# Projection stage of an attention and MLP kernel: Q and K tiles stored directly, weight splitting handed out from one paced list

## The chip, the cores and the metric

One NeuronCore of a Trainium2 chip runs the whole kernel. The metric is the device time of one execution in microseconds. Three runs of the kernel before gave 3447.6, 3449.01 and 3449.11 us, so its median is 3449.01 us.

## The reference, cut to what matters

The input x has 2048 rows of 1024 numbers. It is normalised, goes through an attention block of 32 heads and through an MLP with a Mish activation, and the two results are multiplied:

```python
xn = layernorm(x)
q, k, v = split(xn @ wqkv)                        # 32 heads of 32
s = softmax(q @ k.T * 32**-0.5) @ v, joined @ wo
h = xn @ w1 + b1                                  # 1024 -> 3584
g = silu((h * tanh(softplus(h))) @ w2)            # 3584 -> 1024
out = x + s * g
```

All tensors are float32.

## The kernel before

Every float32 operand of a product is split into a high part, rounded to the type that TensorE multiplies (`F32R`), and a low part, the rest. A product is then three matmuls (`THREE`, line 284). The high part is made by `copy` (line 273, ScalarE, shown as ACT) or by a copy on GpSimd (POOL); the low part by `low` (line 280), a subtraction on VectorE (DVE) or POOL. W2's products also go by sums and differences of its four blocks, seven tiles in place of eight (`w2_parts`, line 655).

The program has three stages before the long one: normalising x and the V projection (lines 368 to 525), then the **Q and K projection** (lines 677 to 719), and after it attention and MLP, whose order on every engine is set by a planner (`Plan`, line 82). The change lies in the Q and K projection alone.

That stage has 16 feature tiles f (even f is Q, odd f is K) with 4 column groups c each. I number the 64 groups as slots, 4f + c. In each slot `qk_group` (line 677) issues 24 matmuls of 128x512 into one PSUM bank, ACT copies the bank to the high half of a tile `st` (shown as qst, two buffers), DVE makes its low half, and ACT's queue stores the 512 KB to DRAM. The store is not issued by `qk_group` itself: it is put on the list `later` (line 49) and issued by `later.tick()` at the end of the same slot. PSUM has eight banks in one ring. From f = 12 on, each slot also has four matmuls of head 0's scores (`s_mm`, line 578), whose row maxima DVE takes.

Beside this, three things go on:

- In slots with c = 0, `qk_split` (line 482) splits the weights of the next f: two copies on ACT and two subtractions on DVE (names qkw). The raw weights for the f after that are loaded by ACT's queue (`qk_load`, line 476).
- In the first 14 f, `w2_parts(f, c)` gives POOL one step of W2's pair u = f: 2, 2, 2 and 1 tiles (`w2_part`, line 649). SP's queue stores each tile (w2s from pw) and, after step 3, loads the raw blocks for u + 2 (`w2_load`, line 645).
- In the first 10 f, at c = 3, `presplit` (line 630) loads half a tile of W1 on SP's queue; two ticks later POOL splits it and SP stores it (w1s from pw). There is one buffer for the raw half (praw) and six for the results (pw).

SP's queue also loads the stacked Q and K of head 0 at slot 32 and of head 1 at slot 57 (`load_head`, line 560, lines 707 to 711). Head 1's tiles take the place of W2's raw blocks (`stacks(early, 1)` and line 646 have the same tags).

Each engine issues its instructions in the order of the code. Across engines the program is emitted in an order that the compiler finds by its own timing of the engines. In that emitted order, every transfer of SP's and ACT's queues takes the next of eight completion semaphores in turn. So a transfer is started only when the eighth transfer ahead of it has landed, unless that one is known to have landed, and whichever queue it was on. In the program before, the store of slot 47 comes eight after the transfer of W2 tile (13, 1), and the store of slot 48 eight after that of tile (13, 6). The last W2 transfer, tile (13, 3), stands between the stores of slots 45 and 46.

Of the kernel before, what the change touches and what calls it, by code (L numbers as in the profile page):

```python
# [20 lines left out]
NC = S // 512  # L21
NT = S // P
FT = F // P
SCALE = DH ** -0.5
EPS = 1e-5

W1_0, W1_V = 4, 23
NS = H * NT
U = FT // 2

# [191 lines left out]
def body(ctx: ExitStack, tc: tile.TileContext, x, wqk, wv, wo, w1, b1, w2, out):  # L222
    nc = tc.nc
# [49 lines left out]
    def copy(out_, in_, scale=1.0):  # L273
        nc.scalar.activation(out_, in_, AF.Copy, scale=scale)  # L274

    def move(out_, in_, eng=None):

        (eng or nc.sync).dma_start(out_.bitcast(F32), in_.bitcast(F32))

    def low(eng, out_, in_, high):  # L280

        eng.tensor_tensor(out_, in_, high.bitcast(F32), ALU.subtract)  # L282
# [10 lines left out]
    later = Later()  # L293
# [148 lines left out]
    for t in range(2, NT + 2):  # L442
# [22 lines left out]
        if t > 7:  # L465
            c, k = t // 4 - 1, t % 4 * 2
# [9 lines left out]
    def qk_load(f):  # L476
        raws[f] = big.tile([P, KT, P], F32, tag="raw", name=f"qkraw{f}")
        (nc.scalar if f > 1 else nc.sync).dma_start(raws[f], wqk[f])
# [3 lines left out]
    def qk_split(f):  # L482
        qkw[f] = w_tile(f"qkw{f}")
        split_w(qkw[f], raws.pop(f))
# [50 lines left out]
    def stacks(pool_, i):  # L535
        stack_pool.append(pool_)
        qst.append(pool_.tile([P, S], F32R, tag=f"qstack{i}", name=f"qstack{i}"))
        kst.append(pool_.tile([P, S], F32R, tag=f"kstack{i}", name=f"kstack{i}"))
        if i == 0:
            nc.gpsimd.memset(qst[i][96:P, :].bitcast(F32), 0.0)  # L540
            move(zeros, qst[i][96:P, :])
            nc.vector.memset(kst[i][96:P, :].bitcast(F32), 0.0)
            nc.vector.memset(kst[i][96:98, :].bitcast(F32), 1.0)
# [16 lines left out]
    def load_head(h, parts=range(3)):  # L560
        r = slice(h % 4 * DH, h % 4 * DH + DH)
        q, k = qst[h % 3], kst[h % 3]
        if h > 2:
            move(q[96:98, :], zeros[0:2, :])
        elif h:
            move(q[96:P, :], zeros)
            move(k[96:P, :], kst[0][96:P, :])
        for i, (a, b) in enumerate(THREE):
            move(q[i * DH:(i + 1) * DH, :], qs[h // 4][a, r, :])
            move(k[i * DH:(i + 1) * DH, :], ks[h // 4][b, r, :])  # L570
# [7 lines left out]
    def s_mm(h, qt, kc):  # L578
        sp_ = ps1.tile([P, 512], F32, tag="ps", name=f"s{h}_{qt}_{kc}")
        nc.tensor.matmul(sp_, qst[h % 3][:, qt * P:(qt + 1) * P],  # L580
                         kst[h % 3][:, kc * 512:(kc + 1) * 512], start=True, stop=True)
        if qt % 4 == 0 and kc == 0:
            negm[h] = early.tile([P, 4, 4], F32, tag=f"mx{qt // 4 % 2}", name=f"mx{h}_{qt}")
        nc.vector.reduce_max(negm[h][:, qt % 4, kc:kc + 1], sp_, axis=AX.X)
        if qt % 4 == 3 and kc == 3 and qt < NT - 1:
            m_tail(h, qt // 4, negm[h])
# [28 lines left out]
    def load_w1(n):  # L615
        w1t[n] = w1p.tile([P, 2, KT // 2, P], F32R, tag="w1", name=f"w1_{n}", bufs=W1S)
        move(w1t[n], w1s[n // 2 % FT][:, n % 2])
# [7 lines left out]
    def pw_tile(name):  # L625
        pw_made.append(name)
        where, tag = ((w1p, "w1"), (sp, "pw"))[len(pw_made) % 2]
        return where.tile([P, 2, 512], F32R, tag=tag, name=name, bufs=3)

    def presplit():  # L630
        f, half = next(jobs)
        raw = sp.tile([P, 512], F32, tag="praw", name=f"praw{f}_{half}", bufs=1)
        nc.sync.dma_start(raw.rearrange("p (k f) -> p k f", f=P), w1[f][:, half * 4:half * 4 + 4])

        def split():
            w = pw_tile(f"pw{f}_{half}")
            nc.gpsimd.tensor_copy(w[:, 0], raw)
            low(nc.gpsimd, w[:, 1], raw, w[:, 0])
            later.at(1, lambda: move(w1s[f][:, half], w.rearrange("p a (k f) -> p a k f", f=P)))

        later.at(2, split)
# [3 lines left out]
    def w2_load(u):  # L645
        raw2[u] = early.tile([P, 4, 512], F32, tag=f"{'qk'[u % 2]}stack1", name=f"raw2_{u}")
        nc.sync.dma_start(raw2[u].rearrange("p (f d) n -> p f (d n)", f=2), w2[u])

    def w2_part(u, j, v):
        w = pw_tile(f"pw2_{u}_{j}")  # L650
        nc.gpsimd.tensor_copy(w[:, 0], v)  # L651
        low(nc.gpsimd, w[:, 1], v, w[:, 0])
        later.at(1, lambda: move(w2s[u][:, j], w))

    def w2_parts(u, step):
        b11, b12, b21, b22 = [raw2[u][:, i] for i in range(4)]
        if step == 0:
            raw2[u, "t"] = sp.tile([P, 512], F32, tag="tmp2", name=f"tmp2_{u}", bufs=1)
        tmp = raw2[u, "t"]

        def minus(a, b, out_):
            nc.gpsimd.tensor_tensor(out_, a, b, ALU.subtract)  # L662
            return out_

        if step == 0:
            w2_part(u, 0, b11)
            w2_part(u, 2, b21)
        elif step == 1:
            w2_part(u, 5, minus(b12, b11, tmp))
            w2_part(u, 1, minus(b22, b12, b12))  # L670
        elif step == 2:
            w2_part(u, 4, minus(b22, tmp, tmp))
            w2_part(u, 6, b22)
        else:
            w2_part(u, 3, minus(b21, tmp, tmp))

    def qk_group(f, c):
        w = qkw[f]
        ps = ps1.tile([P, 512], F32, tag="ps", name=f"qk{f}_{c}")
        n = 0  # L680
        for k in range(KT):
            for a, b in THREE:
                nc.tensor.matmul(ps, w[:, k // 4, a, k % 4], xc[c][:, b, k], start=n == 0, stop=n == 3 * KT - 1)  # L683
                n += 1
        st = sp.tile([P, 2, 512], F32R, tag="qst", name=f"qst{f}_{c}")
        copy(st[:, 0], ps)
        low(nc.vector, st[:, 1], ps, st[:, 0])
        dst = (qs, ks)[f % 2][f // 2].rearrange("h p n -> p h n")[:, :, c * 512:(c + 1) * 512]
        later.at(1, lambda: move(dst, st, nc.scalar))

    w2_load(0)
    w2_load(1)
# [1 line left out]
    for f in range(2 * KT):  # L694
        for c in range(NC):
            qk_group(f, c if f < 2 * KT - 1 else (c + 1) % NC)
            if f < U:
                w2_parts(f, c)
                if c == 3 and f + 2 < U:
                    later.at(1, lambda u=f + 2: w2_load(u))  # L700
            if c == 3 and f < 2 * (FT - W1_V):
                presplit()
            if c == 0 and f + 1 < 2 * KT:
                qk_split(f + 1)
                if f + 2 < 2 * KT:
                    later.at(1, lambda f=f + 2: qk_load(f))
            if f == 8 and c == 0:
                load_head(0)
            if f == 14 and c == 1:
                stacks(early, 1)  # L710
                load_head(1)
            if f >= 12:
                for kc in range(4):
                    s_mm(0, 4 * (f - 12) + c, kc)
            if f == 2 * KT - 1 and c == 1:
                load_w1(0)
                load_w1(1)
            later.tick()
# [23 lines left out]

    total = 2 * 4 * NS * MM + NC * FT * 45 * MM + NS * PV
    slot = total / NS

# [89 lines left out]
    def t_stream():  # L835
        pts = {}
        for T in range(NS):
            h, kt = divmod(T, NT)
# [554 lines left out]
    for c in range(NC):  # L1393
        for s in range(4):
# [3 lines left out]
            for dh in range(2):  # L1398
# [5 lines left out]
                if c:  # L1404
                    n = 2 * s + dh
# [53 lines left out]
```

## Time and profile before

| | |
|---|---|
| median of three runs | 3449.01 us |
| the profiled execution | 3453.82 us |
| its span, first to last instruction | 3452.0 us |
| mean granted TensorE clock | 0.992 |
| PE busy over the span | 3372.2 us (98%) |
| POOL busy over the span | 2794.2 us (81%) |
| first Q and K matmul | 219.90 us |
| last score matmul of the stage | 621.27 us |

PE is TensorE, PEld its weight loads, SPq and ACTq the issuing of transfers on the queues of SP and ACT. "Busy" counts the time of an engine's own instructions; a waiting engine is idle. In a timeline the bracket behind a line gives the idle time ahead of it and the instruction or transfer that ended it. Records start and end with overlaps of about a tenth of a microsecond, since matmuls are pipelined.

### The profile page before, as it was taken

How to read it: one execution, taken by the hardware profiler on the slowest of the kernel's cores; microseconds unless marked ns; L12 is line 12 of the kernel's file. 1: busy time of each engine (PE TensorE's matmuls, PEld its weight loads, DVE VectorE, ACT ScalarE, POOL GpSimd, SP SyncE). 2: the span in 40 equal slices, each digit the busy share in tenths (PEclk: the TensorE clock that was granted, in tenths of full speed). 3: DMA queues.
4: the chain of work that ended last, by engine and by line, in shares of the span. 5: the costliest groups of instructions: out<-in, count | busy, mean ns of one | idle time of the engine just before them, and what ended most of it. 6: DMA issues, size and time to landing. Idle time of an engine off the chain costs nothing.

```text
span 3452.0 us, 48687 instructions
## 1 busy us (share of the span) xinstructions
PE 3372.2 (98%) x17491; PEld 2474.5 (72%) x17491; DVE 2616.3 (76%) x4382; ACT 2017.9 (58%) x3360; POOL 2794.2 (81%) x1033
## 2 busy tenths in 40 slices
PE   8999998999999999999999999999999999999999
PEld 8998777777776667666776676666676666667587
DVE  6012215899999998888989988898999889996753
ACT  6111111576776766676766677666676677677621
POOL 2669891689888989899889889989988999989910
PEclk9999999999999999999999999999999999999999
DMA  9989994444555556545455664445555545546582
GB/s 334 324 303 365 348 354 165 130 139 144 152 157 152 149 167 198 152 127 161 141 150 144 195 182 143 129 138 150 153 152 188 174 138 158 151 154 193 167 308 86
DMA packets 255477, 639.92 MB, mean 185 GB/s; under 512 B 90026, under 2 KB 99242, under 8 KB 244906
## 3 DMA queue, kind: packets, MB, share of 16 engines
q1 hardware_dynamic: 233364, 587.52, 54.7%
q10 hardware_dynamic: 21872, 49.29, 3.9%
q8 instruction: 139, 2.28, 0.3%
q14 instruction: 102, 0.84, 0.1%
HBM read 474.97 MB, written 160.69 MB: 184 GB/s over the span
## 4 chain that ended last, share of the span: by engine, by line
PE 78%; POOL 8%; DVE 7%; DMA 4%; ACT 2%; issue 1%; SPq 0%; ACTq 0%; POOLq 0%; DVEq 0%
PE h L1008 16%; PE y L1149 13%; PE pv L897 12%; PE s L762 12%; PE t L849 12%; PE v L329 4%; PE op L1276 4%; POOL pw L282 3%; PE qk L683 2%; DVE mx L768 2%; POOL pw L651 1%; POOL tmp L662 1%; POOL z L878 1%; DMA praw<-in_B_w_dram 1%; DVE yacc L1172 1%
## 5 line engine op out<-in xcount | busy, mean ns | idle before, releaser
L878 POOL TENSOR_TENSOR z<-z,p 128x2048 f32<-128x2048 f32 x448 | 2067.2, 4614 | 75.8 <-ACT p L271 51.4
L271 ACT ACTIVATE p<-t,zero 128x512 f32<-128x512 f32 x2048 | 1365.9, 689 | 459.4 <-PE t L849 438.9
L768 DVE TENSOR_REDUCE mx<-s 128x1 f32<-128x512 f32 x1984 | 1281.3, 680 | 69.6 <-PE s L762 66.9
L849 PE MATMUL t<-qstack,kstack 128*128 128x512 f32 x2048 | 792.1, 394 | 2.1 <-ACT p L271 0.9
L762 PE MATMUL s<-kstack,qstack 128*128 128x512 f32 x1984 | 756.7, 398 | 16.3 <-DMA kstack<-ks 4.8
L1008 PE MATMUL h<-xr,w 128*128 128x512 f32 x2016 | 678.1, 391 | 1.6 <-DVE aw L282 0.6
L1172 DVE TENSOR_TENSOR yacc<-yacc,y 128x512 f32<-128x512 f32 x728 | 491.2, 678 | 39.6 <-PE y L1149 36.4
L762 PEld LDWEIGHTS s<-kstack,qstack 128*128 128x128 f32 x1984 | 367.7, 188 | 162.0 <-issue 29.9
L849 PEld LDWEIGHTS t<-qstack,kstack 128*128 128x128 f32 x2048 | 382.0, 188 | 127.2 <-issue 28.5
L897 PE MATMUL pv<-p,v 128*32 128x512 f32 x4096 | 467.0, 596 | 0.9 <-ACT p L271 0.6
L1008 PEld LDWEIGHTS h<-xr,w 128*128 128x128 f32 x2016 | 378.6, 188 | 84.7 <-DVE aw L282 2.1
L683 PE MATMUL qk<-xc,qkw 128*128 128x512 f32 x1536 | 362.5, 397 | 12.5 <-ACT qkw L274 9.0
L683 PEld LDWEIGHTS qk<-xc,qkw 128*128 128x128 f32 x1536 | 293.7, 192 | 78.5 <-ACT qkw L274 10.7
L878 POOL TENSOR_TENSOR z<-p,p 128x2048 f32<-128x2048 f32 x32 | 147.7, 4617 | 231.2 <-ACT p L271 120.7
L897 PEld LDWEIGHTS pv<-p,v 128*32 128x32 f32 x4096 | 120.1, 110 | 277.4 <-issue 247.9
L282 DVE TENSOR_TENSOR qst<-qk,qst 128x512 fp32r<-128x512 f32 x64 | 44.2, 691 | 283.0 <-ACT qst L274 283.0
L274 ACT ACTIVATE qst<-qk 128x512 fp32r<-128x512 f32 x64 | 38.3, 598 | 345.7 <-PE qk L683 120.5
L1149 PE MATMUL y<-w,az 128*128 128x512 f32 x672 | 232.3, 395 | 5.7 <-POOL az L282 2.7
L1149 PE MATMUL y<-w,ay 128*128 128x512 f32 x672 | 228.1, 393 | 3.4 <-ACT ay L274 1.3
L1149 PE MATMUL y<-w,ax 128*128 128x512 f32 x672 | 225.6, 392 | 3.1 <-DMA w<-w2s 1.1
L1008 PE MATMUL h<-xc,w 128*128 128x512 f32 x672 | 225.3, 391 | 0.0
L329 PE MATMUL v<-vw,xc 128*128 128x256 f32 x1536 | 192.6, 286 | 5.8 <-DVE xc L282 3.7
(123 smaller groups left out, 3662.9 us busy)
## 6 DMA issues: line engine op xcount, KB each, us to landing
w<-w2s SPq DMA_DIRECT2D x392, 512.0 KB
w<-w1s SPq DMA_DIRECT2D x224, 512.0 KB
w2s<-pw SPq DMA_DIRECT2D x98, 512.0 KB
qstack<-qs SPq DMA_DIRECT2D x96, 256.0 KB
kstack<-ks SPq DMA_DIRECT2D x96, 256.0 KB
x<-in_A_x_dram SPq DMA_DIRECT2D x32, 512.0 KB
qs<-qst ACTq DMA_DIRECT2D x32, 512.0 KB
ks<-qst ACTq DMA_DIRECT2D x32, 512.0 KB
```

Source lines behind the costliest of these rows:

```text
L271: nc.scalar.activation(out_, in_, fn, bias=zero if bias is None else bias, scale=scale)
L282: eng.tensor_tensor(out_, in_, high.bitcast(F32), ALU.subtract)
L329: nc.tensor.matmul(ps[:, :256], xc[t // 4][:, a, k, (t % 4) * P:(t % 4 + 1) * P], w[:, b, k], start=n == 0, stop=n == 3 * KT - 1)
L683: nc.tensor.matmul(ps, w[:, k // 4, a, k % 4], xc[c][:, b, k], start=n == 0, stop=n == 3 * KT - 1)
L762: nc.tensor.matmul(sp_, qst[h % 3][:, qt * P:(qt + 1) * P], kst[h % 3][:, kc * 512:(kc + 1) * 512], start=True, stop=True)
L768: nc.vector.reduce_max(tiles["mx"][:, qt, kc:kc + 1], tiles[qt, kc], axis=AX.X)
L849: nc.tensor.matmul(tp, kst[h % 3][:, kt * P:(kt + 1) * P], qst[h % 3][:, c * 512:(c + 1) * 512], start=True, stop=True)
L878: nc.gpsimd.tensor_tensor(zs[h], pts[T - 1] if kt == 1 else zs[h], pts[T], ALU.add)
L897: nc.tensor.matmul(t["b"][c * DH:(c + 1) * DH, :], vt[h][:, k, :], pts[T - kt + k][:, c * 512:(c + 1) * 512], start=k == kt - size + 1, st ...
L1008: nc.tensor.matmul(t["h"], w1t[m_][:, a, k % 4], xts_[c][:, b, k], start=i == 0, stop=i == 3 * KT - 1)
L1149: nc.tensor.matmul(t["y"], acts[B, kind][:, p, half * 256 + s * P:half * 256 + (s + 1) * P], w2t[m_][:, q], start=i == 0, stop=i == 2)
L1172: nc.vector.tensor_tensor(ya, ya, t["y"], ALU.subtract)
```

## The change

The store of a Q or K tile is issued in `qk_group`, straight behind the copy and the subtraction, and no longer at the tick. W2's steps and W1's halves stand in one list `todo`, each with a place, its running cost over `PACE` = 1.85: a step costs its number of tiles, a half of W1 costs 1. In a slot all jobs are taken whose place is at or before the slot's number. The cost is 14 x 7 + 10 = 108 in all, so the last job falls due by slot 58; before, the last step was at slot 55. Head 1's loads move from slot 57 to slot 60.

```diff
+PACE = 1.85
...
+    todo, cost = [], 0.0
+    for u in range(U):
+        for step, n in enumerate((2, 2, 2, 1)):
+            def job(u=u, step=step):
+                w2_parts(u, step)
+                if step == 3 and u + 2 < U:
+                    later.at(1, lambda: w2_load(u + 2))
+            todo.append((cost / PACE, job))
+            cost += n
+        if u < 2 * (FT - W1_V):
+            todo.append((cost / PACE, presplit))
+            cost += 1
...
-        later.at(1, lambda: move(dst, st, nc.scalar))
+        move(dst, st, nc.scalar)
...
-            if f < U:
-                w2_parts(f, c)
-                if c == 3 and f + 2 < U:
-                    later.at(1, lambda u=f + 2: w2_load(u))
-            if c == 3 and f < 2 * (FT - W1_V):
-                presplit()
+            while todo and todo[0][0] <= f * NC + c:
+                todo.pop(0)[1]()
...
-            if f == 14 and c == 1:
+            if f == 15 and c == 0:
                 stacks(early, 1)
                 load_head(1)
```

## Rows read from the trace of the kernel before

**Rows 1.** Busy time by stretch: engines, granted clock, DMA share, GB/s.

```profile
core 0: us, PE busy (x) PEld busy (x) DVE busy (x) ACT busy (x) POOL busy (x), PEclk, DMA share, GB/s
226.96:530.02 303.06, 278.25 (x1179) 225.27 (x1178) 65.47 (x78) 41.45 (x73) 281.90 (x272) 0.96 0.96 347
538.46:621.11 82.65, 82.65 (x366) 68.43 (x365) 43.80 (x78) 10.40 (x21) 0.00 (x0) 1.00 0.37 124
...
275.00:300.00 25.00, 25.00 (x112) 20.70 (x111) 6.00 (x7) 3.56 (x7) 23.96 (x24) 1.00 1.02 394
```

**Rows 2.** Timeline of PE: start, length, line, operation [idle before, and what ended it].

```profile
219.90 152.51 PE L683 MATMUL qk<-xc,qkw 128*128 128x512 f32 x672
...
525.41 0.80 PE L580 MATMUL s<-kstack,qstack 128*128 128x512 f32 x1 [6.64 <-DVE qst L282]
...
529.44 8.28 PE L683 MATMUL qk<-xc,qkw 128*128 128x512 f32 x24
...
538.46 5.60 PE L683 MATMUL qk<-xc,qkw 128*128 128x512 f32 x24
...
544.81 5.60 PE L683 MATMUL qk<-xc,qkw 128*128 128x512 f32 x24
...
620.20 1.07 PE L580 MATMUL s<-kstack,qstack 128*128 128x512 f32 x4
```

**Rows 3.** Waits from 226 to 531 us: waiter, releaser, total, times, longest.

```profile
ACT qst L274 <- DMA w2s<-pw: 77.9, 13, 9.7
ACT qst L274 <- DMA ks<-qst: 61.0, 11, 11.6
...
PE s L580 <- DVE qst L282: 9.7, 2, 6.6
PE qk L683 <- ACT qkw L274: 9.0, 4, 4.0
...
POOL pw L651 <- DMA w2s<-pw: 5.8, 1, 5.8
...
POOL pw L637 <- DMA praw<-in_B_w_dram: 3.0, 3, 1.9
```

**Rows 4.** Timeline of ACT and of its queue, about slots 44 and 48.

```profile
494.47 0.60 ACT L274 ACTIVATE qst<-qk 128x512 fp32r<-128x512 f32 x1 [6.20 <-DMA w2s<-pw]
494.97 1.14 ACT L274 ACTIVATE qkw<-qkraw 128x512 fp32r<-128x512 f32 x2
502.03 0.40 ACTq L278 DMA_DIRECT2D ks<-qst  x1
...
524.03 0.60 ACT L274 ACTIVATE qst<-qk 128x512 fp32r<-128x512 f32 x1 [6.84 <-DMA w2s<-pw]
524.53 1.14 ACT L274 ACTIVATE qkw<-qkraw 128x512 fp32r<-128x512 f32 x2
528.97 0.37 ACTq L278 DMA_DIRECT2D qs<-qst  x1
```

**Rows 5.** Timeline of POOL: the list's first job and its end.

```profile
226.96 1.00 POOL L651 CAST pw<-raw 128x512 fp32r<-128x512 f32 x1 [16.06 <-DVE qst L282]
...
524.70 1.27 POOL L282 TENSOR_TENSOR pw<-raw,pw 128x512 fp32r<-128x512 f32 x1
...
528.74 1.28 POOL L282 TENSOR_TENSOR pw<-tmp,pw 128x512 fp32r<-128x512 f32 x1
```

**Rows 6.** Timeline of DVE behind slot 48's copy.

```profile
525.27 2.92 DVE L282 TENSOR_TENSOR qkw<-qkraw,qkw 128x512 fp32r<-128x512 f32 x2
528.11 2.47 DVE L584 TENSOR_REDUCE mx<-s 128x1 f32<-128x512 f32 x4
```

**Rows 7.** Timeline of SP's queue: head 0's loads, and W2's last stores.

```profile
398.67 0.73 SPq L278 DMA_DIRECT2D qstack<-qs  x1
...
413.15 1.84 SPq L278 DMA_DIRECT2D w2s<-pw  x2
...
492.98 37.38 SPq L278 DMA_DIRECT2D w2s<-pw  x14
```

## The prediction

> **What bounds the kernel now.** I read the busy time by stretch first, to find where PE is not full, then PE's timeline, then the waits of that stretch, then ACT's, POOL's, DVE's and SP's timelines at its end. PE is the bound over the whole span, so a microsecond that PE loses in the Q and K stage is a microsecond of the kernel. From 538 us on PE is full with a DMA share of 0.37; while POOL works on its list, from 226.96 to 530.02, PE has 278.25 of 303.06 us and the DMA share is 0.96 [rows 1]. The stage loses its time under the list.
>
> How much: 28 groups in 152.51 us make 5.447 us each, and with four score matmuls a slot takes 544.81 - 538.46 = 6.35 us [rows 2]. Undisturbed, 48 x 5.447 + 16 x 6.35 = 363.0 us would lead from 219.90 to 582.9. The stage ends at 620.20 + 1.07 = 621.3 [rows 2]: **38.4 us are lost**, all before 538.
>
> What takes them: PE waits little by name, 9.0 us for split weights and 9.7 for a freed bank, but ACT waits 77.9 us, in 13 places, on transfers of W2 tiles, and 61.0 on stores of K [rows 3]. A Q or K store neither reads nor writes W2's tiles; what ties them is the turn of the eight semaphores. So ACT can't be further than POOL's list lets it, and PE, eight banks ahead at most, stands still when ACT does. ACT evacuates slot 44 at 494.47 [rows 4] (counted back from the last evacuation); undisturbed that would be 219.90 + 45 x 5.447 = 465.0. It is 29.5 us late. Slot 48 is copied at 524.03 [rows 4], PE goes on at 525.41, starts slot 50 at 529.44 and never waits again [rows 2]. The list's last product ends at 530.02 [rows 5]. The end of the stage is therefore the list's end, plus the slots that stand behind it in the emitted order.
>
> **Is the list held by the slots?** This decides the change. POOL's 303.06 us hold 281.90 of work [rows 1]; of the other 21.2, waits make 5.8 + 3.0 = 8.8 [rows 3], and the gaps between 272 instructions 12.4. No wait is on ACT, DVE or PE once the list has started. (The wait ahead of the first job, 16.06 us [rows 5], I put down to the load of its raw data: the code gives that job nothing to wait for on DVE.) And W2's last 14 stores, which the code puts in slots 48 to 55, start at 492.98 [rows 7], when ACT is at slot 44 [rows 4]: POOL is four slots ahead of the place at which the code gives it the work. The code's slots do not hold POOL; its own 294 us of work and gaps do. A list with other due slots gives POOL the same instructions in nearly the same order, and the compiler's timing again lets it run ahead.
>
> **The change part by part.**
>
> *Store at once, c other than 0 (48 or 49 slots).* Between copy and tick ACT has no other work there: 0. In four slots with f of 12 or more a small copy of the row maxima now follows the store and not the reverse; PE needs it no sooner than nine ticks later: 0.
>
> *Store at once, c = 0 (15 slots).* The two copies for the next weights, 1.14 us, used to go ahead of the store; now they stand behind it, and behind its wait. The raw load behind them moves too, by nothing that was not there. Cover: the weights are needed three slots later, 16.3 us. Where ACT is later than that, the cover is gone, as at slots 44 and 48. At slot 44 the store starts at 502.03 and the copies at 494.97 [rows 4], so the copies would come up to 7.4 us later; PE would start slot 48 that much later, but slots 49 and 50 must wait for ACT's evacuations anyway, so it is hidden under the stand at 525.41. At slot 48 it is not hidden: DVE must split those weights (2.92 us) before it takes the maxima of slot 48 [rows 6], and the bank of that maximum is what PE waits for ahead of slot 50. Upper end: the copies start at 528.97 + 0.37 and not at 524.53 [rows 4], +4.8 us. Lower end: the store finds its semaphore free and waits for DVE's half alone, to about 525.35, +1.2. Below that there is nothing, since the copies went first before. The store, emitted sooner, should stand one or two transfers further ahead and so wait for the W2 tile before: 281.90 us of work over 108 tiles and halves are 2.6 us each. I take 4.8 - 2.6 = **+2.2**.
>
> The Trainium skill (DMA: Bandwidth & Descriptors, "Issuing engines are not separate DMA queues") says that the engine on which a transfer is started saves only the sequencer's time to start it, small beside the transfer. By it this part is worth 0 and the sum 2.2 lower; the rows disagree, since a start here was held for 3.6 us and for 6.2 while its own record takes 0.4.
>
> *The paced list.* The work is the same 98 W2 tiles and 10 halves of W1: 0 for POOL's 294 us. Its 8.8 us of waits can fall: a half of W1 is split up to a slot later after its load (3.0 us at stake); head 0's loads stand between two other W2 stores on SP's queue. They held W2's stores from 398.67 to 413.15 [rows 7] and through them POOL for 5.8. They still stand among W2's stores, about six tiles sooner, so I keep the 5.8 and take the 3.0 away: **-3.0**, ends -8.8 and 0.
>
> *Head 1's loads.* On SP's queue they stand behind all W2 stores before and after, with nothing between: 0.
>
> *Order of the transfers.* Which W2 transfer stands eight ahead of a given store changes. If the list ends one slot sooner or later among the stores, one slot more or fewer is left behind it: 6.35 us either way, unknown in sign; I take 0. Bytes and matmuls are unchanged.
>
> Sum: 2.2 - 3.0 = -0.8 against the profiled execution's 3453.82 us (span 3452.0 and 1.8 around it). That execution is 4.8 above the median, so the forecast is 3449.01 - 0.8 = **3448.2 us**. About 0.2%, or 6.9 us, is what a measurement of this kernel can tell from no change.
>
> **The rivals.**
>
> *The pace holds.* If the emitted order does follow the due slots, the list ends behind slot 58, and each store stands behind W2 tiles that POOL finished long ago. 58.4 slots are 48 x 5.447 + 10.4 x 6.35 = 327.5 us, for 294 of POOL. For it: 38.4 us lie there to be had. Against it: POOL's lead over the code. The DMA engines would limit it: they moved 347 GB/s at a share of 0.96 [rows 1], 361 at a full one; 303.06 us at 347 are 105.2 MB, ten more stores and two weight loads of 0.52 MB make 111.4, over 327.5 us 340 GB/s, a share of 0.94. At such shares waits remain; I leave a quarter, 10 us: 3449 - 28 = **3421**, between 3411 and 3430. Where 394 GB/s were moved (1.02) [rows 1], PE did not stop yet.
>
> *ACT's queue becomes the stop: slower.* At c = 0 the store's wait now holds the next weights. If the stand at 525.41 does not hide slot 44's 7.4 us, PE comes to slot 48 late as well: 7.4 + 4.8 = 12.2, **3461**; with one more group at a low clock (the first after the stand took 8.28 and not 5.60 us [rows 2]) 3464. It decides from the point at which ACT is over 16.3 us late, which it was, 29.5, at slot 44. Against it: PE's banks are full there, so it would have stood anyway.
>
> *Nothing moves.* If the compiler's order comes out the same but for single places, the terms above shrink to the first one: 3449 to 3452, inside the forecast.
>
> **How the numbers follow.** Forecast's mechanism, own range 3440 to 3458 (the terms' ends and a slot either way, not all at once): 0.60; of it 0.44 lies within 0.2%, 0.10 below, 0.06 above. Pace holds: 0.20. ACT's queue stops PE: 0.15. Something else: 0.05, near even. Faster 0.32, the same 0.44, slower 0.24. The range that should hold it 8 times in 10 goes into both rivals: 3422 to 3463.
>
> **What would show it.** Right: POOL's list again takes 300 us or so without waits on ACT or PE; ACT's waits on w2s stay near 78 us; the stage ends within a slot of 621; the qkw copies of slot 48 start behind its store. The pace holds, if the list ends near 545 us and ACT's waits on w2s go below 30. The rival on ACT's queue, if PE's wait for qkw grows from 9.0 to over 20 and the stage ends beyond 630. If another stage than this one changes by over 3 us, I have missed a coupling.

## The result, and the profile after

The changed kernel takes **3463.9 us**, the median of five runs (3462.05 to 3466.74), against 3449.11 us of the kernel before beside it. The ratio is 1.0043 with a 95% interval of 1.0028 to 1.0058: **slower by 14.8 us, 0.43%**. I had forecast 3448.2 us and no change, and the range ended at 3463. The profiled execution took 3463.9 us, its span is 3462.1.

Busy time by stretch of the changed kernel: the first stretch is POOL's list from its first job to its end, the second the slots behind it. It answers to [rows 1].

```profile
core 0: us, PE busy (x) PEld busy (x) DVE busy (x) ACT busy (x) POOL busy (x), PEclk, DMA share, GB/s
226.85:534.51 307.66, 276.77 (x1177) 224.81 (x1175) 64.03 (x72) 42.58 (x72) 280.57 (x272) 0.95 0.93 342
547.30:630.30 83.00, 83.00 (x369) 68.75 (x367) 43.62 (x76) 10.83 (x22) 0.00 (x0) 1.00 0.32 116
```

POOL's work is what it was, 272 instructions and 280.57 us, but the list takes 307.66 us where it took 303.06. PE now leaves 307.66 - 276.77 = 30.9 us of the stretch empty, before 24.8. Behind the list PE is full again.

PE's timeline of the changed kernel about slot 48, and its end of the stage (start, length; in brackets the idle time ahead and what ended it). It answers to [rows 2].

```profile
527.45 0.80 PE L582 MATMUL s<-kstack,qstack 128*128 128x512 f32 x1 [4.58 <-DVE qst L284]
531.61 0.80 PE L582 MATMUL s<-kstack,qstack 128*128 128x512 f32 x1 [3.37 <-DVE qst L284]
537.83 0.79 PE L582 MATMUL s<-kstack,qstack 128*128 128x512 f32 x1 [5.42 <-DVE mx L586]
538.42 8.33 PE L698 MATMUL qk<-xc,qkw 128*128 128x512 f32 x24
...
629.24 1.07 PE L582 MATMUL s<-kstack,qstack 128*128 128x512 f32 x4
```

Slot 50 starts at 538.42, 9.0 us later than at 529.44, and the stage ends at 630.3, 9.0 us later than at 621.3. The last stand before it (a wait of PE), 5.42 us for a row maximum, is one that I had named. In the kernel before it was 2.64 us:

```profile
528.84 0.79 PE L580 MATMUL s<-kstack,qstack 128*128 128x512 f32 x1 [2.64 <-DVE mx L584]
```

Two parts make the 9.0. **The list ends later**: its last product starts at 533.25 and takes 1.26, so it ends at 534.51 and not at 530.02, +4.5:

```profile
533.25 1.26 POOL L284 TENSOR_TENSOR pw<-tmp,pw 128x512 fp32r<-128x512 f32 x1
```

**The tail is longer**: from the list's end to the stage's end 95.8 us, before 91.25, +4.55. The two need different causes, and the next two views have them.

Waits of the changed kernel from 226 to 535 us (waiter, releaser, total, times, longest), as [rows 3].

```profile
ACT qst L276 <- DMA w2s<-pw: 68.3, 14, 7.3
...
PE qk L698 <- ACT qkw L276: 18.6, 4, 6.9
...
ACT qst L276 <- DMA w1s<-pw: 14.2, 1, 14.2
POOL pw L639 <- DMA praw<-in_B_w_dram: 13.8, 4, 5.3
...
ACT qkw L276 <- DMA w2s<-pw: 9.6, 2, 7.2
...
POOL pw L653 <- DMA w1s<-pw: 1.0, 1, 1.0
```

POOL's wait for the raw half of W1 is 13.8 us where it was 3.0; its wait of 5.8 for a W2 store is gone and 1.0 for a W1 store has come. Waits of 8.8 us have become 14.8. ACT's weight copies now wait on W2's transfers themselves, 9.6 us; no such line stood there before.

Timelines of the changed kernel at slot 48, ACT and its queue, then DVE; they answer to [rows 4] and [rows 6].

```profile
530.24 0.60 ACT L276 ACTIVATE qst<-qk 128x512 fp32r<-128x512 f32 x1 [3.57 <-DMA w2s<-pw]
534.77 0.39 ACTq L280 DMA_DIRECT2D qs<-qst  x1
535.21 1.15 ACT L276 ACTIVATE qkw<-qkraw 128x512 fp32r<-128x512 f32 x2 [4.38 <-DMA w2s<-pw]
...
535.88 1.29 DVE L284 TENSOR_TENSOR qkw<-qkraw,qkw 128x512 fp32r<-128x512 f32 x2 [4.32 <-ACT qkw L276]
537.09 2.48 DVE L586 TENSOR_REDUCE mx<-s 128x1 f32<-128x512 f32 x4
```

The copies start at 535.21, 0.44 us behind the store and 4.97 behind the evacuation; before it was 0.50 behind the evacuation (524.03 to 524.53). DVE can take the weights' low half only then, and the row maximum at 537.09 after that.

### The profile page after: what moved, and what is told of

The parts are those of the page before. It is cut to its first block, busy times and chain, and to the rows that moved or that the text cites. A ratio compares the mean times of both kernels' runs of the same rounds, so it can differ in the third digit from the quotient of the medians.

```text
span 3462.1 us, 48685 instructions
## 1 busy us (share of the span) xinstructions
PE 3371.6 (97%) x17491; PEld 2473.6 (71%) x17491; DVE 2619.2 (76%) x4382; ACT 2020.3 (58%) x3360; POOL 2792.6 (81%) x1033
## 5 line engine op out<-in xcount | busy, mean ns | idle before, releaser
L773 PE MATMUL s<-kstack,qstack 128*128 128x512 f32 x1984 | 755.8, 397 | 15.6 <-DMA kstack<-ks 5.9
L698 PE MATMUL qk<-xc,qkw 128*128 128x512 f32 x1536 | 362.5, 397 | 20.8 <-ACT qkw L276 18.6
```

The lines of the kernel that those rows point to most:

```text
L773: nc.tensor.matmul(sp_, qst[h % 3][:, qt * P:(qt + 1) * P], kst[h % 3][:, kc * 512:(kc + 1) * 512], start=True, stop=True)
```

## The experiments

Twelve runs were made, one of them of the kernel before once more. Each time stands beside the kernel before on the same chip. For the table I split the stage's time at the list's end in each profile: "list" is from the start of POOL's first tile to the end of its last, "tail" from there to the end of the stage's last score matmul.

| kernel | time, us (before beside it) | ratio, 95% interval | list | tail | span behind the stage |
|---|---|---|---|---|---|
| before | 3449.11 | | 303.06 | 91.25 | 2830.7 |
| before, second profile | 3448.67 (3450.14) | 0.9990 to 1.0008 | 302.06 | 92.37 | 2826.2 |
| changed | 3463.90 (3449.11) | 1.0028 to 1.0058 | 307.66 | 95.80 | 2831.8 |
| store at once alone | 3454.07 (3448.33) | 1.0005 to 1.0024 | 300.87 | 94.88 | 2828.8 |
| store at once, c = 0 | 3454.19 (3450.14) | 1.0002 to 1.0020 | 300.35 | 95.07 | 2826.4 |
| store at once, c = 1, 2, 3 | 3450.52 (3450.14) | 0.9993 to 1.0011 | 301.84 | 90.89 | 2825.9 |
| list alone | 3458.25 (3448.33) | 1.0018 to 1.0039 | 310.62 | 91.25 | 2829.9 |
| changed, half of W1 first | 3451.61 (3448.33) | 1.0001 to 1.0019 | 299.54 | 94.48 | 2829.1 |

### The two parts apart

The store alone, in the kernel before:

```diff
-        later.at(1, lambda: move(dst, st, nc.scalar))
+        move(dst, st, nc.scalar)
```

> Only the store is moved; W2 and W1 are handed out as before. Theory (the emitted order ties the stores to POOL's list, and the list's end sets the stage's end): POOL's list ends as before, near 530 us, with some 9 us of waits; the copies of slot 48's weights stand behind its store's wait, so PE goes on some 4.5 us later than before. Stage end near 626, time 3452 to 3456 us, a third of the whole loss. Rival (stores started at once crowd W2's transfers, and that is the whole loss): 3462 to 3466 us with the list ending near 534. Second rival (the store is harmless, the list is all): 3449 us, stage end 621.

3454.07 us, +5.7 (1.7 to 8.3 by the interval), as expected. In the profile the list is shorter and the tail longer than before: the list ends at 527.1 us and not near 530, the stage at 622.0 and not near 626. PE's last stand is the changed kernel's, 5.42 us for a row maximum.

The list alone, in the changed kernel:

```diff
-        move(dst, st, nc.scalar)
+        later.at(1, lambda: move(dst, st, nc.scalar))
```

> Only the list is paced; the store stays at the tick. Theory: W1's raw halves stand behind W2's raw blocks on SP's queue in some places, POOL waits 10 us or more for them, the list ends near 534.5 us, the stage near 626, time 3453 to 3459 us. Rival (the store is the whole loss): 3449 us, list end near 530. Second rival (the list is the whole loss): 3462 to 3466 us.

3458.25 us, +9.9 (6.2 to 13.4), as expected, with the list ending at 537.7 and the stage at 629.0, both 3 us later than I had said. The tail is that of before, 91.25 (the second profile of the kernel before has 92.37); the list is 310.62 us. Together the two parts give +15.6, the change +14.8: within their intervals they add up, so each part can be explained by itself.

### The list: what stands ahead of the half of W1

SP's queue in the kernel before, and in the changed kernel, at the same half (praw), the same raw blocks of W2 (raw) and the W2 store ahead of them (w2s); below each, POOL as it takes that half:

```profile
287.17 0.88 SPq L633 DMA_DIRECT2D praw<-in_B_w_dram  x1
...
290.02 0.32 SPq L278 DMA_DIRECT2D w2s<-pw  x1
290.38 0.90 SPq L647 DMA_DIRECT2D raw<-in_B_w_dram  x1
...
294.12 1.07 POOL L637 CAST pw<-praw 128x512 fp32r<-128x512 f32 x1
```

```profile
284.83 5.53 SPq L280 DMA_DIRECT2D w2s<-pw  x3
...
290.40 0.43 SPq L649 DMA_DIRECT2D raw<-in_B_w_dram  x1
290.88 0.79 SPq L635 DMA_DIRECT2D praw<-in_B_w_dram  x1
...
298.74 0.61 POOL L639 CAST pw<-praw 128x512 fp32r<-128x512 f32 x1 [4.86 <-DMA praw<-in_B_w_dram]
```

In the code before, both loads were due at c = 3, the half at once and W2's blocks one tick later. In the list the half has its own place behind step 3, often a slot later, and six of its ten loads now start behind the 1 MB of W2's blocks and the W2 store ahead of those, which SP holds until POOL has made its tile. POOL, which takes its jobs in the emitted order, reached four of these six halves before they had landed. At the half shown, the store is started by 290.4 us in both kernels. Before, the half's load had started ahead of it, and POOL came for the half 6.95 us after that start without a wait. Now the load starts 3.7 us later, at 290.88, and POOL comes at 293.88, only 3.0 us after the start, and waits 4.86: the half takes 7.86 us to land. So most of this wait is the later start; of the transfer itself, at most some 1 us more than the 6.95 that were enough before, the 1 MB may be the reason, which no run shows by itself. The test puts the half ahead of step 3, and so ahead of both, in the changed kernel:

```diff
         for step, n in enumerate((2, 2, 2, 1)):
+            if step == 3 and u < 2 * (FT - W1_V):
+                todo.append((cost / PACE, presplit))
+                cost += 1
...
-        if u < 2 * (FT - W1_V):
-            todo.append((cost / PACE, presplit))
-            cost += 1
```

> The changed kernel with each W1 half put ahead of W2's step 3 in the list, so that its raw load is issued ahead of the 1 MB load of W2's raw blocks. Same work. Theory: POOL's waits for these halves fall from 13.8 to under 5 us, the list ends 6 to 10 us sooner (525 to 529), and the stage with it: 3454 to 3458 us. Rival (the waits for the halves are not on the path, POOL's lateness is made up later): as the changed kernel, 3462 to 3466 us.

3451.61 us, some 12 us of the 14.8 back and more than I had expected. All ten halves go ahead of the raw blocks again. Waits from 226 to 527 us of this kernel:

```profile
POOL pw L639 <- DMA praw<-in_B_w_dram: 5.6, 1, 5.6
...
POOL pw L653 <- DMA w1s<-pw: 1.0, 1, 1.0
```

The wait is down to one of 5.6 us, at 407 us, with head 0's loads ahead of the half on SP's queue. The list takes 299.54 us, 8.1 less than in the changed kernel, while the tail keeps its 94.48.

### The store: which slots carry its cost

In the kernel before, stored at once only where c = 0, and only where it is not (the line of the diff above under `if first:`, and under `if not first:`, with the old line in the other branch):

> Before, with the store at once in the slots with c = 0 alone (there the two weight copies then stand behind the store and its wait), at the tick elsewhere. Theory A (the cost of storing at once lies in these copies: they hold DVE's halves of the weights, those hold the row maxima, and PE waits for the bank): all of the cost of the run with the store alone, +4 to +7 us against before, and PE's wait for a row maximum near 5.4 us as there. Theory B (the cost lies in the changed order of all the transfers): 0 to +2 us.

> Before, with the store at once in the slots with c = 1, 2, 3, at the tick where c = 0. Theory A: ACT has nothing between copy and tick there, so nothing changes: within 2 us of before, PE's wait for a row maximum as before (2.6 us). Theory B: +4 to +6 us.

+4.1 us (0.7 to 6.9) and +0.4 us (-2.4 to 3.8), beside the same runs of the kernel before. PE's last stands before slot 50, first with c = 0 at once, then with the others at once:

```profile
530.95 0.80 PE L580 MATMUL s<-kstack,qstack 128*128 128x512 f32 x1 [5.42 <-DVE mx L584]
```

```profile
527.64 0.80 PE L580 MATMUL s<-kstack,qstack 128*128 128x512 f32 x1 [2.65 <-DVE mx L584]
```

The cost is in the slots with c = 0, where the weight copies stand behind the store. Over all profiles of kernels without the gate that comes below, the tail is 91.4 us with these stores at the tick (four profiles, 90.89 to 92.37) and 95.3 with them at once (six, 94.48 to 95.93, two of them further down): **+3.9**. Theory B, the order of the transfers, does not fit these tails and stands. But the loss is not all seen in the stage: with the store at once alone, and with c = 0 alone, the list is shorter and the stage ends at 622.0 and 622.7 us, only 0.2 and 0.9 behind the 621.8 that the two profiles of the kernel before have on the mean, where the medians are 5.7 and 4.1 longer.

> The kernel before, once more, for a second profile of it: the first came from an execution 4.7 us above the median. If that surplus lies in the Q and K stage (transfers that meet otherwise from one execution to the next), a profile at the median shows the stage ending near 617 us and the rest as before; if it lies elsewhere, the stage ends near 621 again. As a kernel: the same time as before, within 2 us.

The second profile of the kernel before comes from an execution 1.8 us above its median and ends its stage at 622.4, not near 617: the 4.7 us by which the first execution was above its median do not show in the stage.

### What the pace would be worth: a gate

My rival "the pace holds" needed POOL to follow the slots, which the code does not make it do. So I made it: DVE copies one column of a slot's low half into a small tile, and POOL copies that column before it takes the slot's jobs.

```diff
+    token = early.tile([P, 64], F32, name="token")
+    gate = early.tile([P, 1], F32, name="gate")
...
         low(nc.vector, st[:, 1], ps, st[:, 0])
+        nc.vector.tensor_copy(token[:, 4 * f + slot:4 * f + slot + 1], st[:, 1, 511:512].bitcast(F32))
...
+            if todo and todo[0][0] <= f * NC + c:
+                nc.gpsimd.tensor_copy(gate, token[:, 4 * f + c:4 * f + c + 1])
             while todo and todo[0][0] <= f * NC + c:
```

> The changed kernel, and POOL is held to the slots: DVE writes one column of a token behind each slot's low half, and POOL copies it ahead of the slot's jobs (some 50 added instructions of 128x1 on POOL, 64 on DVE). The emitted order then has the list's end behind slot 58 and every store ahead of the W2 tiles of its own slot. Theory: ACT's waits on W2 transfers nearly vanish, PE's stands too; the stage ends between 583 and 602 us, time 3420 to 3437 us. Rival (the DMA engines are the bound, 0.95 busy under the list): ACT's waits turn into waits on its own stores, stage end near 620, 3445 to 3455 us. Second rival (the token makes POOL wait for slots and the list ends late, head 1's loads with it): a new stand behind the stage, gain under 10 us.

3448.25 us, ratio 0.9991 to 1.0008: no faster than before, where I had expected 3420 to 3437. But the stage ended at 583.9 us, 46 earlier than in the changed kernel, and PE did not stand in it. 30 to 36 us were lost behind the stage: 2862.1 us of span there, where all kernels of the table have 2826 to 2832. What differs there is the place of tiles: `token` and `gate` stand in a pool with the stacks of Q and K, and the stacks of heads 0 and 2 and the stage's buffers moved by 288 bytes (the tiles' own 260, rounded up). The next four kernels take this apart. In the first the column lies in `pad2`, a tile of 48 columns that is there already:

```diff
-    nc.vector.memset(early.tile([P, 48], F32, name="pad2"), 0.0)
+    pad2 = early.tile([P, 48], F32, name="pad2")
+    nc.vector.memset(pad2, 0.0)
...
+        i = slot % 40
+        nc.vector.tensor_copy(pad2[:, i:i + 1], st[:, 1, 511:512].bitcast(F32))
...
+            if todo and todo[0][0] <= slot:
+                nc.gpsimd.tensor_copy(pad2[:, 47:48], pad2[:, slot % 40:slot % 40 + 1])
```

> After, with the gate as in the run before (POOL takes a slot's jobs only behind that slot's low half, through one column that DVE copies), but the columns lie in the 48-column tile that stands there already, so no tile's place in SBUF moves. Theory A (the gate removes the stands, and what the first gate lost behind the stage, 33 us, came from the 260 bytes by which its two new tiles moved everything behind them): the stage ends near 584 again and the rest is as in the changed kernel, 3463.9 - (630.3 - 583.7) = 3417 us, down to 3448.3 - (621.3 - 583.7) = 3411; matmuls behind the stage come every 0.2265 us again. Theory B (a PE that has not stood in the stage runs the rest slower, or the emitted order of the rest changed): the stage ends near 584 and the time stays near 3448, matmuls behind the stage every 0.232 us.

> After, with the two tiles of the first gate (64 columns and 1 column) allocated at the same place and cleared once by DVE, and no gate. Theory A (the place of the tiles costs the time): the stage ends near 630 as in the changed kernel, and the rest loses some 33 us: 3463.9 + 33 = 3497 us, at least 3490. Theory B (the place does not matter): 3463.9 us, within 4.

The gate in `pad2`: **3419.37 us**, ratio 0.9906 (0.9891 to 0.9920), with the stage ending at 587.1. The two tiles without a gate: 3493.91 us against 3452.14, 0.0082 of a ratio above the changed kernel, some 28 us, with the stage ending at 631.1, as in the changed kernel. The gate is worth the stage's time and the tiles cost what it had given back.

> Before, with the gate of e5_gate_pad at its own slots (W2's steps at 4u + c, halves of W1 at c = 3), the store at the tick. Theory A (POOL's lead over the code is what costs the 38 us, the even pace costs or gives little): the stage ends at 583 to 592, PE waits for little, 3411 to 3420 us. Theory B (the even pace is needed as well: eight tiles in four slots of 21.8 us are 20.8 us of POOL's work, and with the halves of W1 POOL falls behind the slots again): stage end 600 to 615, 3428 to 3443 us.

3416.04 us, ratio 0.9899 (0.9884 to 0.9914): the old list at its old slots, gated, does as well as the even one. The pace of 1.85 is not needed once POOL can't run ahead.

> e5_gate_pad with the store back at the tick, so that in slots with c = 0 the weight copies stand ahead of the store again. Theory A (a store costs the copies behind it only what it waits, and under the gate it waits for next to nothing): as e5_gate_pad within 3 us. Theory B (storing at once costs by itself, 4 to 6 us as in the run with the store alone): 4 to 6 us faster than e5_gate_pad.

**3414.20 us, ratio 0.9886 (0.9869 to 0.9902): the lowest median, and faster than both kernels**; the gated old list is not told apart from it. It is 5.2 us below the gate with the store at once, whose four runs all lie above these four. Theory B's number came, with theory A's place: there the gate does not make the c = 0 stores free. It can, though: in the profile of the first gate, which stores at once too, PE does not stand at slot 50 and needs 364.3 us for the stage. PE at slot 50 with the store at once, then PE in the whole stage with it at the tick:

```profile
495.57 0.50 PE L582 MATMUL s<-kstack,qstack 128*128 128x512 f32 x1 [2.02 <-DVE mx L586]
496.16 7.34 PE L698 MATMUL qk<-xc,qkw 128*128 128x512 f32 x24
```

```profile
core 0: us, PE busy (x) PEld busy (x) DVE busy (x) ACT busy (x) POOL busy (x), PEclk, DMA share, GB/s
219.90:583.80 363.90, 363.90 (x1612) 301.58 (x1610) 129.90 (x228) 54.89 (x99) 291.48 (x326) 1.00 0.91 329
```

At once, PE stands 2.02 us for the same row maximum as in the changed kernel, and the group behind it takes 7.34 us and not 5.60; from the first Q and K matmul to the last score matmul it needs 367.3 us. At the tick it needs 363.0, which is 48 x 5.447 + 16 x 6.35: PE is full at a granted clock of 1.00.

## Why the prediction was wrong, and where it was right

**What bounds the stage: right.** The list takes 307.7 us, without waits on ACT or PE, and the stage's end follows its end. The gated kernels show the other side: take POOL's lead away and the stage ends at 582.5 to 583.9 in three of them and at 587.1 in the fourth, where I had put the undisturbed one at 582.9. Of the 38.4 lost us, only part is idle time; the Q and K matmuls are also shorter without stands. The group of these matmuls in the changed kernel, then with the gate and the store at the tick (busy us, mean ns | idle before, and what ended it):

```profile
L698 PE MATMUL qk<-xc,qkw 128*128 128x512 f32 x1536 | 362.5, 397 | 20.8 <-ACT qkw L276 18.6 <-DVE qkw L284 2.2
```

```profile
L698 PE MATMUL qk<-xc,qkw 128*128 128x512 f32 x1536 | 350.9, 389 | 0.0
```

11.6 us of the gain lie in these matmuls, which no longer run below a granted clock of 1.00 (the stretch of the list has 0.95, the gated stage 1.00); behind a stand, 24 of them took 8.33 us at 538.42, and 5.60 later.

**The paced list: wrong, and the step that failed.** I took 3.0 us away, with 0 as the upper end ("its 8.8 us of waits can fall: a half of W1 is split up to a slot later after its load"). I looked at the distance from the load to its use and not at what stands ahead of the load on SP's queue. In six of ten cases that is now the 1 MB of W2's raw blocks and the store that they stand behind, so the load starts later and the distance on which I had counted is gone: 3.0 us and not 6.95 at the half shown above. The wait that was to go from 3.0 to 0 went to 13.8; the 5.8 that I kept is gone, with 1.0 in its place. Waits: 14.8 - 8.8 = +6.0. The list by itself: 310.62 - 302.3 = +8.3 with the store at the tick (302.3 is the mean of 303.06, 302.06 and 301.84), 307.66 - 300.6 = +7.1 with it at once. And by the runs +9.9. With the half ahead the list is 299.54, 1.1 below the 300.6 of the old list with the store at once, and one wait of 5.6 for a half is left: even there the 3.0 that I took away did not come. I had followed head 0's loads and head 1's past the other transfers of SP's queue, and not this one.

**The store at once, c = 0: right in mechanism, too small in size.** +2.2 lay between the ends 1.2 and 4.8, by a credit of 2.6 for a store that would wait for one W2 tile less. That credit did not come: in the emitted order the store of slot 48 still comes eight after the transfer of tile (13, 6), as before, and it starts at 534.77, past the list's end at 534.51. The tail is 3.9 us longer, inside my ends. I was wrong to read the sentence of the Trainium skill (DMA: Bandwidth & Descriptors, "Issuing engines are not separate DMA queues") as a price of 0 for this part, and wrong that the rows disagree with it. It speaks of what starting transfers on several engines at once saves. The store is started on ACT's queue before and after, and what costs is the wait ahead of its start: 4.38 us of ACT's idle time at slot 48 ended with a W2 transfer which ACT had not started. No run here tests the sentence. What came besides, and I had not foreseen, is a list 1.7 us shorter (300.6, the mean of 300.87 and 300.35, against 302.3), which I can't explain.

**The store at once elsewhere: right**, 0 forecast, +0.4 us measured with an interval that holds 0.

**The rival "ACT's queue becomes the stop"** gave 3461 to 3464, and 3463.9 came, with the stage ending beyond 630 as it said. Its price is not what happened. It put 7.4 us on slot 44, and PE did wait for those weights, 6.32 us ahead of 508.09; but the store alone has the same wait, 8.42 us, and does not end its stage later for it (622.0). The changed kernel, then the store alone:

```profile
508.09 8.21 PE L698 MATMUL qk<-xc,qkw 128*128 128x512 f32 x24 [6.32 <-ACT qkw L276]
```

```profile
500.58 7.37 PE L683 MATMUL qk<-xc,qkw 128*128 128x512 f32 x24 [8.42 <-ACT qkw L274]
```

The stand was taken off the next ones, as I had said against that rival. Its other 4.8 us are the forecast's own upper end, 3.9 measured. The rest of the number is the list's, which no rival of mine had: that this rival's number came is chance.

**The rival "the pace holds"** was rightly held unlikely for this change and rightly priced: 3421, 3411 to 3430; the gated kernels give 3419, 3416 and 3414. The quarter that I left for busy DMA engines was not needed with the store at the tick: PE is full at a share of 0.91.

**My signs.** Two held (the list's waits, the copies behind the store) and one in part: ACT waits on W2's stores for 68.3 us instead of 78, but 14.2 on a W1 store have come. "The stage ends within a slot of 621" failed, with 630.3, and PE's wait for qkw is 18.6 us, just short of the 20 that I had set for the rival. Whether another stage changed by over 3 us is not decided: behind the stage the changed kernel has 2831.8 us, the two profiles of the kernel before 2830.7 and 2826.2.

**What stays open.** The profiles put 8 to 9 of the 14.8 us in the stage: it ends at 621.3 and 622.4 in the two profiles of the kernel before, at 630.3, 631.1 and 629.7 in the changed kernel and the two that differ from it by dead tiles alone. The span behind the stage is 2826 to 2832 us in all kernels of the table, without an order to it (2836 in the profile of the gated old list, an execution 4.7 us above its median). Against the mean of the two (621.8) the medians of the other kernels of the table are 2.5 to 6.3 us further from before than their stages are, most where the c = 0 stores go at once (3.2 to 6.3). Both profiles of the kernel before come from executions above their medians, by 4.7 and 1.8 us, those of the others from executions up to 3.3 us off theirs on either side. The intervals are 6 to 10 us wide, and no run here tells this from scatter.

## What to carry to other kernels

When a load is moved, write down the transfers that stand ahead of it on its queue before and after, and what those wait for: a small load that comes to stand behind them starts when they have started, and the time that is left until its use shrinks (here from 6.95 us to 3.0). An engine that works ahead of the code is not paced by where the code puts its jobs; a wait on the data of the slot is what paces it, and here that was worth about 1% in three kernels. A number that comes out as a rival said shows nothing of the rival's cause until its parts are measured one by one.

## What the runs showed of the hardware

**The place of tiles in SBUF changes the pace of the matmuls.** With 288 bytes per partition added, the span behind the stage is 30 us longer, 2862.0 against 2831.8. The kernels with and without the dead tiles have the same instructions in the same order on every engine, apart from the clearing of the tiles; only addresses differ. Busy time from 700 to 3300 us, first of the kernel with the dead tiles, then of the changed kernel:

```profile
700.00:3300.00 2600.00, 2572.19 (x13093) 1772.92 (x13092) 2299.96 (x3842) 1805.66 (x2977) 2332.88 (x633) 1.00 0.53 155
```

```profile
700.00:3300.00 2600.00, 2568.38 (x13209) 1789.59 (x13208) 2315.59 (x3853) 1806.13 (x2983) 2353.73 (x641) 1.00 0.53 157
```

In the same 2600 us, as busy and at the same granted clock of 1.00, PE has 116 matmuls fewer on record. The groups of h<-xr, whose operands were not moved, show it, 395 ns against 391, as those of the scores do (400 against 397); pv, with 32 columns of weights, does not (596 and 596). Again the dead tiles first:

```profile
L1024 PE MATMUL h<-xr,w 128*128 128x512 f32 x2016 | 685.8, 395 | 1.3 <-DVE aw L284 0.6 <-DVE yacc L1188 0.6
```

```profile
L1019 PE MATMUL h<-xr,w 128*128 128x512 f32 x2016 | 678.3, 391 | 1.4 <-DVE aw L284 0.6 <-DMA xr<-xs 0.4 <-DVE yacc L1183 0.3
```

The last kernel moves the same tiles by 256 bytes and not by 288:

```diff
+    dead = early.tile([P, 64], F32, name="dead")
+    nc.vector.memset(dead, 0.0)
```

> After, with one dead tile of 64 columns, 256 bytes in each partition, in the place where e6_dead_tiles had its two; there the stacks of heads 0 and 2 and the Q and K stage's buffers moved by 288 bytes, here by 256. Theory A (what costs is that tiles lie off a multiple of 64 bytes: 288 is none, 256 is one): as the changed kernel, 3463.9 us within 4. Theory B (any move of these tiles, or any further tile, costs): 3490 to 3498 us, as in e6_dead_tiles.

3462.14 us, ratio 1.0029 to 1.0062, as the changed kernel, with 2827.2 us behind the stage. So it is not that tiles were moved but where they came to stand; 288 is no multiple of 64 (nor of 128 or 256), and two sizes do not tell which of these counts. At the end of the attention, matmuls whose own operands stand where they stood are slow only beside others whose operands moved. In the kernel with the dead tiles h<-xr takes 394 ns from 3128 to 3206 us, beside the score products (t) of the last head but one, whose stacks moved; from 3208 to 3285, beside those of the last head alone, whose stacks did not move, it takes 391, and the changed kernel has 390 and 391 there:

```profile
L1024 PE MATMUL h<-xr,w 128*128 128x512 f32 x102 | 34.6, 394 | 0.0
```

```profile
L1024 PE MATMUL h<-xr,w 128*128 128x512 f32 x97 | 29.3, 391 | 0.0
```

Why they slow down there is not known. Whoever adds a small tile to a tuned kernel should look at the matmuls far behind it.
